# First-batch head pairs on the casting queue, and w_out with two rows to a partition

## The chip, the core and the metric

The kernel runs on one NeuronCore of a Trainium2 chip. Times are device microseconds (us) of that core. The kernel before was timed in 7 runs: median 297.09 us, lowest 295.44, highest 298.5. The profile shows one execution of its own, which took 297.81 us; its span, from the first to the last instruction that the profiler records, is 296.0 us.

## What is computed

Attention with 16 extra "beacon" keys that every query sees, then a feed-forward block with a product instead of a non-linearity, over 8 batches, 8 heads of width 64 and 576 positions:

```python
B, H, S, Nb, D = (8, 8, 576, 16, 64)
k_all = np.concatenate([beacon_k, k], axis=2)
v_all = np.concatenate([beacon_v, v], axis=2)
scores = scale * np.matmul(q, k_all.transpose(0, 1, 3, 2))
causal[:, Nb:] = np.triu(np.ones((S, S), dtype=bool), k=1)
a = np.exp(scores - scores.max(-1)) ; a /= a.sum(-1) + 1e-09
x = matmul(a, v_all).transpose(0, 2, 1, 3).reshape(B * S, H * D)     # 4608 x 512
out = ((x @ w1) * (x @ w2) @ w3) @ w_out                             # DF = 1024
```

Inputs and output are float32 in HBM; the kernel multiplies in float16. Since nothing stands between `w3` and `w_out`, the kernel forms their product once (`Wt`, 1024 x 512) and multiplies by that.

## The kernel before

**One list sets everything.** The string `ORDER` is a list of some 1,200 small operations. The last loop of the kernel goes through it and calls a function for each word, under a manual schedule: each engine executes its instructions exactly in the order in which the list gives them, and semaphores hold only what depends on other engines. So the list is also the order of the DMA queues. There is no planner at build time.

**The words.** `lq b c`, `lk b c`, `lkb b`, `lv b c`, `lvb b` load queries, keys, beacon keys, values, beacon values of batch b. `l1 c`, `l2 c`, `l3 r`, `lo a` load pieces of w1, w2, w3 and w_out; each piece is 512 KB of float32 in HBM and 256 KB as float16 on the chip. `t3 r` transposes a block of 128 rows of w3 on the PE, `e3` copies it out of PSUM, `f r a` multiplies it with piece a of w_out (two matmuls of 512 columns), and after `f r 0` to `f r 3` `ew r` writes block r of `Wt`. `tq`/`tk` are PE transposes of queries and keys, `eq`/`ek` their copies out, `tn`/`en` the same for the beacon keys of batch 0, `s b g` the scores of group g (13 to a batch), `exp` the exponential, `m` the causal mask, `v` the product with the values, `n` the division, `x`/`ex` a PE transpose of the attention output and its copy, `TX` the same by a transposing DMA. `Dq`/`Dk` are transposing DMAs of queries and keys, used from batch 2 or 3 on. `a`, `b` are x @ w1 and x @ w2, `ea` and `eb` their copies and product, `o` the product with `Wt`, `eo` its copy, `st` the store. `spin n` issues n matmuls on zeros, whose result is not used.

**Two queues of loads.** [...] Loads on the POOL queue write float16 from float32. At most eight POOL loads are under way: each waits for the landing of the one eight before it. The two queues share the 16 DMA engines.

**Batch 0 is loaded differently.** A head pair c (heads 2c and 2c+1) of q or k comes as one transfer of 96 partitions, each with six consecutive positions of both heads. In the kernel before all eight such transfers (`lq 0 c S`, `lk 0 c S`, 288 KB each) are float32 on SP, into the eight slots of `st8`, one slot each (`NOWN` = 8). `cast` on DVE (line 394) turns a slot into float16 with the heads side by side, `tq`/`tk` (line 406) then need six transposes to a pair. Slots 4 to 7 serve one more purpose: the first 128 columns of each hold the transposed block 2 of w3 (`HELD`, lines of `wT`), from `e3 2` until `f 2 0` to `f 2 3` have read slots 4, 5, 6, 7 in turn. So the last four pairs, `lk 0 2`, `lk 0 3`, `lq 0 2`, `lq 0 3`, stand in the list behind these, one by one.

**What is asked for at the start.** Before the first `f` the list issues on SP: `lq 0 0`, beacon keys, `lk 0 1`, `lk 0 0`, `lq 0 1`; and on POOL, behind the preparation of an identity and two masks: beacon values, `lo 0`, `lo 1`, `l3 0`, `l3 1`, `l3 2`, `l3 5`, `lo 2`, `lo 3`, `l3 3`.

Of the kernel before, what the change touches and what calls it, by code (L numbers as in the profile page):

```python
# [9 lines left out]
FP16 = mybir.dt.float16  # L10
AF = mybir.ActivationFunctionType
ALU = mybir.AluOpType
ds, ts = bass.ds, bass.ts
# [49 lines left out]
consts 0; consts 1; consts 2; spin 8 7; lq 0 0 S; lkb 0; lk 0 1 S; lk 0 0 S; lq 0 1 S; lvb 0; lo 0;  # L63
lo 1; cast 0 0 q; castb A; l3 0; tq 0 0 6; tn 0 7; cast 0 1 k; l3 1; eq 0 0 A 6; en 0 D 7; l3 2;
tk 0 1 5; cast 0 0 k; l3 5; ek 0 1 A 5; spin 1 7; tk 0 0 6; lo 2; ek 0 0 A 6; lo 3; spin 3 7;
s 0 0 0; s 0 1 2; s 0 2 4; exp 0 0 0; cast 0 1 q; spin 1 7; tq 0 1 6; exp 0 1 2; m 0 0 0; l3 3;
eq 0 1 D 6; exp 0 2 4; m 0 0 1; spin 3 7; s 0 3 0; s 0 4 2; lv 0 1; exp 0 3 0; spin 1 7; s 0 5 4;
spin 2 7; t3 0 6; l3 4; exp 0 5 4; m 0 1 0; e3 0 D 6; exp 0 4 2; spin 2 7; t3 1 7; lv 0 4; m 0 1 1;
f 0 0 6; e3 1 D 7; f 0 1 6; lv 0 0; t3 2 5; f 1 0 7; e3 2 A 5; f 1 1 7; lv 0 3; t3 5 4; f 2 0 5;
e3 5 A 4; f 2 1 5; lk 0 2 S; lv 0 2; f 2 2 5; lk 0 3 S; f 5 0 4; lq 0 2 S; f 1 2 7; f 2 3 5; l1 1;  # L70
f 0 2 6; ew 2 A 5; lq 0 3 S; f 0 3 6; f 5 1 4; ew 0 A 6; l3 6; t3 3 5; f 5 2 4; e3 3 A 5;
cast 0 2 k; f 5 3 4; f 1 3 7; lk 1 4 P; ew 5 D 4; tk 0 2 6; ew 1 A 7; f 3 0 5; ek 0 2 D 6; f 3 1 5;
f 3 2 5; cast 0 3 k; f 3 3 5; tk 0 3 6; l2 3; ew 3 A 5; cast 0 2 q; t3 4 7; ek 0 3 A 6; tq 0 2 4;
e3 4 D 7; lq 1 0 P; eq 0 2 A 4; spin 1 5; f 4 0 5; cast 0 3 q; s 0 6 0; s 0 7 2; l3 7; exp 0 6 0;
f 4 1 5; lq 1 1 P; tq 0 3 6; f 4 2 5; exp 0 7 2; eq 0 3 D 6; v 0 0 1 7; l2 1; m 0 2 0; v 0 0 0 6;
n 0 0 1 7; v 0 2 0 4; s 0 8 0; s 0 9 2; l1 0; n 0 2 0 4; exp 0 8 0; v 0 1 1 7; n 0 0 0 6; f 4 3 5;
lq 1 4 P; n 0 1 1 7; exp 0 9 2; t3 6 6; lk 1 1 P; tk 1 4 4; ew 4 D 5; s 0 10 0; e3 6 A 6;
v 0 1 0 7; ek 1 4 D 4; s 0 11 2; s 0 12 4; lkb 1; n 0 1 0 7; exp 0 10 0; f 6 0 6; m 0 2 1; l2 2;
tq 1 0 7; f 6 1 6; m 0 3 0; exp 0 11 2; eq 1 0 D 7; f 6 2 6; v 0 2 1 7; lv 1 3; exp 0 12 4;
m 0 3 1; t3 7 3; n 0 2 1 7; lq 1 2 P; v 0 3 0 2; e3 7 A 3; v 0 3 1 5; n 0 3 0 2; tq 1 1 7; f 6 3 6;  # L80
l1 2; n 0 3 1 5; eq 1 1 A 7; x 0 0 4; x 0 4 3; ew 6 A 6; f 7 0 2; ex 0 0 D 4; x 0 2 7; ex 0 4 D 3;
x 0 1 6; lq 1 3 P; ex 0 2 A 7; x 0 3 5; ex 0 1 D 6; tq 1 4 4; f 7 1 2; ex 0 3 A 5; eq 1 4 D 4;
lk 1 0 P; f 7 2 2; tk 1 1 6; a 0 1 7; l2 0; ek 1 1 A 6; l1 3; f 7 3 2; ea 0 1 A 7; b 0 4 6;
ew 7 D 2; lk 1 2 P; a 0 0 7; lk 1 3 P; tq 1 2 5; ea 0 0 A 7; b 0 2 4; lk 2 0 P; eq 1 2 D 5;
a 0 2 7; lv 1 2; a 0 4 5; lv 1 0; ea 0 2 A 7; eb 0 2 4; tq 1 3 7; lv 1 1; tk 1 0 3; eq 1 3 A 7;
a 0 5 2; ek 1 0 D 3; b 0 0 7; lk 2 2 P; b 0 1 4; eb 0 0 7; lvb 1; a 0 6 3; eb 0 1 4; lq 2 2 P;
tk 1 2 7; ea 0 4 A 5; ea 0 5 D 2; a 0 3 4; lkb 2; ek 1 2 A 7; ea 0 6 D 3; tk 1 3 5; lq 2 3 P;
b 0 5 7; eb 0 4 6; ek 1 3 A 5; ea 0 3 D 4; lk 2 1 P; s 1 0 0; s 1 1 2; s 1 2 4; eb 0 5 7;
exp 1 0 0; lv 1 4; b 0 6 6; lq 2 0 P; exp 1 1 2; m 1 0 0; a 0 7 7; eb 0 6 6; lk 2 3 P; exp 1 2 4;
tk 2 2 3; m 1 0 1; b 0 3 6; lq 2 4 P; ek 2 2 D 3; ea 0 7 A 7; lv 2 2; s 1 3 0; s 1 4 4; s 1 5 2;  # L90
eb 0 3 6; exp 1 3 0; lq 2 1 P; tk 2 0 7; tq 2 3 6; ek 2 0 D 7; exp 1 4 4; s 1 6 0; lk 2 4 P;
eq 2 3 D 6; v 1 0 0 7; m 1 1 0; lk 3 3 P; tk 2 1 6; n 1 0 0 7; exp 1 5 2; v 1 0 1 5; lv 2 1;
ek 2 1 D 6; v 1 1 0 4; tq 2 2 7; n 1 0 1 5; exp 1 6 0; Dk 2 3; tq 2 0 6; lv 2 3; tq 2 4 3; b 0 7 2;
n 1 1 0 4; eq 2 4 A 3; lk 3 0 P; eq 2 2 A 7; m 1 2 0; s 1 7 0; s 1 8 4; eq 2 0 D 6; exp 1 7 0;
lq 4 4 P; tq 2 1 3; m 1 1 1; v 1 2 0 7; lkb 3; eq 2 1 D 3; tk 2 4 6; exp 1 8 4; s 1 9 0; lq 3 2 P;
n 1 2 0 7; v 1 1 1 3; eb 0 7 2; o 0 3 7; lq 3 1 P; exp 1 9 0; n 1 1 1 3; lv 2 0; ek 2 4 A 6;
m 1 2 1; lvb 2; s 1 10 4; s 1 11 0; s 1 12 2; m 1 3 0; eo 0 3 A 7; lq 3 0 P; exp 1 10 4; v 1 3 0 6;
Dk 3 3; o 0 1 7; n 1 3 0 6; st 0 3 P; exp 1 12 2; lv 2 4; Dk 3 0; lq 3 3 P; exp 1 11 0; x 1 0 6;
eo 0 1 D 7; x 1 4 5; v 1 2 1 4; Dq 3 2; lk 3 4 P; ex 1 0 A 6; ex 1 4 D 5; o 0 2 3; n 1 2 1 4;
st 0 1 P; Dq 3 1; m 1 3 1; lk 3 2 P; v 1 3 1 7; eo 0 2 A 3; s 2 0 0; s 2 1 4; s 2 2 2; n 1 3 1 7;  # L100
lvb 3; exp 2 0 0; o 0 0 6; Dq 3 0; st 0 2 P; exp 2 1 4; m 2 0 0; lk 3 1 P; exp 2 2 2; x 1 3 7;
m 2 0 1; x 1 2 5; x 1 1 4; ex 1 3 D 7; s 2 3 0; s 2 4 2; lv 3 1; ex 1 2 D 5; ex 1 1 A 4; v 2 0 0 7;
eo 0 0 D 6; exp 2 4 2; a 1 3 5; n 2 0 0 7; exp 2 3 0; a 1 1 6; Dq 3 3; lq 3 4 P; ea 1 3 D 5;
s 2 5 2; s 2 6 4; s 2 7 0; ea 1 1 A 6; m 2 1 0; lv 3 4; Dk 3 4; exp 2 6 4; v 2 1 0 7; b 1 1 6;
lv 3 2; n 2 1 0 7; exp 2 5 2; m 2 2 0; v 2 0 1 5; eb 1 1 6; v 2 2 0 7; exp 2 7 0; a 1 4 4; Dk 3 2;
lv 3 3; n 2 0 1 5; b 1 3 6; n 2 2 0 7; lv 3 0; ea 1 4 A 4; m 2 1 1; s 2 8 2; s 2 9 0; s 2 10 4;
lq 4 0 P; eb 1 3 6; exp 2 8 2; v 2 1 1 7; b 1 0 6; exp 2 9 0; Dk 3 1; m 2 2 1; lk 4 1 P; n 2 1 1 7;
a 1 0 3; exp 2 10 4; m 2 3 0; a 1 6 7; lkb 5; ea 1 0 D 3; v 2 2 1 5; eb 1 0 6; Dq 3 4; lq 4 2 P;
ea 1 6 A 7; v 2 3 0 4; n 2 2 1 5; a 1 7 6; lq 4 3 P; n 2 3 0 4; b 1 4 7; x 2 0 5; lk 4 3 P;
eb 1 4 7; x 2 4 4; a 1 5 3; ex 2 0 A 5; ex 2 4 D 4; ea 1 7 A 6; b 1 5 7; ea 1 5 D 3; lk 4 0 P;  # L110
s 2 11 0; s 2 12 4; s 3 0 2; eb 1 5 7; st 0 0 P; exp 2 11 0; Dq 4 4; b 1 6 6; lq 4 1 P; exp 3 0 2;
m 2 3 1; b 1 7 7; lkb 4; Dk 4 1; eb 1 6 6; exp 2 12 4; a 1 2 3; m 3 0 0; eb 1 7 7; Dq 4 2;
v 3 0 0 6; ea 1 2 A 3; s 3 1 0; s 3 2 4; s 3 3 2; n 3 0 0 6; exp 3 1 0; Dq 4 3; v 2 3 1 7; b 1 2 6;
exp 3 3 2; m 3 0 1; lv 4 3; Dq 4 0; n 2 3 1 7; s 3 4 0; s 3 5 2; lk 4 2 P; exp 3 2 4; m 3 1 0;
x 2 3 7; eb 1 2 6; lv 4 0; Dk 4 3; exp 3 5 2; x 2 1 5; x 2 2 4; ex 2 3 D 7; o 1 3 6; lk 4 4 P;
ex 2 1 D 5; ex 2 2 A 4; m 3 1 1; lvb 4; exp 3 4 0; lv 4 4; a 2 2 7; eo 1 3 D 6; Dq 4 1; lk 5 0 P;
s 3 6 2; s 3 7 4; s 3 8 0; ea 2 2 A 7; st 1 3 P; Dk 4 0; exp 3 6 2; v 3 0 1 6; a 2 0 7; lv 4 2;
n 3 0 1 6; exp 3 8 0; o 1 1 3; m 3 2 0; ea 2 0 D 7; exp 3 7 4; lq 5 3 P; m 3 2 1; tk 4 2 6;
eo 1 1 A 3; v 3 2 0 7; ek 4 2 D 6; v 3 1 1 5; lk 5 1 P; n 3 2 0 7; a 2 1 6; n 3 1 1 5; Dk 4 4;
st 1 1 P; v 3 1 0 7; ea 2 1 A 6; lv 4 1; s 3 9 0; s 3 10 2; s 3 11 4; n 3 1 0 7; exp 3 9 0;  # L120
lq 5 0 P; b 2 0 6; exp 3 10 2; m 3 3 0; o 1 2 7; eb 2 0 6; exp 3 11 4; v 3 2 1 6; m 3 3 1;
eo 1 2 A 7; v 3 3 0 5; n 3 2 1 6; st 1 2 P; b 2 2 7; n 3 3 0 5; b 2 1 6; eb 2 2 7; TX 3 0;
s 3 12 0; s 4 0 2; s 4 1 4; eb 2 1 6; exp 3 12 0; Dq 5 3; a 2 5 7; exp 4 0 2; v 3 3 1 6;
ea 2 5 D 7; Dk 5 1; s 4 2 0; s 4 3 2; lv 5 0; exp 4 1 4; m 4 0 0; b 2 5 7; n 3 3 1 6; lk 6 3 P;
TX 3 4; exp 4 3 2; m 4 0 1; v 4 0 0 5; a 2 6 6; lk 5 4 P; eb 2 5 7; exp 4 2 0; TX 3 1; lv 5 1;
m 4 1 0; a 2 4 4; ea 2 6 D 6; lk 5 2 P; v 4 1 0 7; n 4 0 0 5; TX 3 3; ea 2 4 A 4; s 4 4 2; s 4 5 0;
s 4 6 4; lv 5 3; n 4 1 0 7; exp 4 4 2; a 2 7 6; Dq 5 0; lq 5 4 P; exp 4 6 4; lvb 5; v 4 0 1 7;
ea 2 7 D 6; lq 5 2 P; b 2 7 3; TX 3 2; exp 4 5 0; n 4 0 1 7; lq 5 1 P; b 2 6 6; m 4 2 0; Dk 5 0;
m 4 1 1; v 4 2 0 7; lk 5 3 P; eb 2 7 3; b 2 4 5; Dk 5 4; n 4 2 0 7; a 2 3 4; eb 2 4 5; lv 5 2;
o 1 0 7; eb 2 6 6; ea 2 3 A 4; Dk 5 2; lq 6 3 P; b 2 3 6; eo 1 0 A 7; s 4 7 0; s 4 8 2; s 4 9 4;  # L130
eb 2 3 6; lq 6 2 P; exp 4 7 0; o 2 2 7; Dq 5 4; st 1 0 P; exp 4 8 2; exp 4 9 4; v 4 1 1 6; m 4 2 1;
eo 2 2 D 7; s 4 10 0; s 4 11 2; s 4 12 4; Dq 5 2; exp 4 10 0; n 4 1 1 6; st 2 2 P; o 2 1 7;
m 4 3 0; Dk 6 3; exp 4 12 4; exp 4 11 2; a 3 2 6; Dq 5 1; eo 2 1 D 7; a 3 4 5; st 2 1 P; m 4 3 1;
ea 3 2 A 6; Dk 5 3; a 3 1 6; ea 3 4 A 5; a 3 0 7; ea 3 1 A 6; b 3 4 6; v 4 3 1 5; Dq 6 3; eb 3 4 6;
# [56 lines left out]
def kernel(  # L191
# [13 lines left out]
    nc = tc.nc  # L205
    B, H, S, D = q.shape
# [475 lines left out]
```

## Time and profile before

| | |
|---|---|
| timed, median of 7 (lowest to highest) | 297.09 us (295.44 to 298.5) |
| profiled execution: time / span | 297.81 us / 296.0 us |
| busy DVE, ACT, POOL | 53%, 55%, 45% of the span |
| scores start on PE | 9.72 us |
| first product with the values (L523) | 34.42 us |
| first w1/w2 product (L564) | 46.58 us on the chain |
| last matmul record / end of span | 292.96 us / 296.0 us |
| HBM read / written | 39.32 MB / 9.44 MB |

PE is TensorE, PEld its weight loads, DVE VectorE, ACT ScalarE, POOL GpSimd, SP the queue of SyncE. Under "timeline" the profile lists instructions with their start; under "chain" it follows back from the last instruction what released each step; under "windows" it sums the busy time of each engine in a stretch, beside the TensorE clock that was granted there (1.00 is full) and what the DMA engines moved. A PE that is marked busy isn't necessarily useful: the `spin` matmuls (line 605) count too, and matmuls at half clock count double.

### The profile page before, as it was taken

Reading aid. Unit: us, or ns where it says so; the run is one execution under the profiler, and the core shown is the slowest. Engines: PE = TensorE matmul, PEld = TensorE weight load, DVE = VectorE, ACT = ScalarE, POOL = GpSimd, SP = SyncE. Lnnn points to the kernel's source line nnn. Section 1 sums busy time; section 2 is a strip of 40 time slices with the busy share of each in tenths; the row PEclk is TensorE's granted clock in tenths of the full one; section 3 lists DMA queues with packets and bytes.
Section 4 is the critical chain, followed back from the end, with each engine's and each line's share of the span. In section 5 each row is a group of like instructions: output and inputs, shape, how many; then the busy total and the mean of one; then the engine's idle time right before and its main releaser. Section 6 shows DMA issues by size and latency. Waiting matters only on the chain.

```text
span 296.0 us, 7052 instructions
## 1 busy us (share of the span) xinstructions
PE 287.8 (97%) x2914; PEld 157.4 (53%) x2914; DVE 156.1 (53%) x350; ACT 162.8 (55%) x211; POOL 133.0 (45%) x185
## 2 busy tenths in 40 slices
PE   7997999999999999999999999999999999999995
PEld 2453675565655556555545554565456444544443
DVE  5323582776677665773526655556676262430430
ACT  3653594498785886657436651765187233443232
POOL 8464688959865385583087820572001000201000
PEclk9998999999999999999999999999999999999999
DMA  7999999999999999999999995699923110331004
GB/s 173 204 191 243 191 172 169 148 140 85 181 174 136 179 129 174 131 128 158 186 195 138 168 168 145 72 149 174 123 70 103 27 38 0 112 86 71 35 30 150
DMA packets 153616, 39.56 MB, mean 134 GB/s; under 512 B 143216, under 2 KB 150128, under 8 KB 153584
## 3 DMA queue, kind: packets, MB, share of 16 engines
q0 software_dynamic: 114320, 26.86, 101.6%
q1 hardware_dynamic: 39264, 12.25, 27.8%
q8 instruction: 23, 0.38, 0.6%
q14 instruction: 9, 0.07, 0.1%
HBM read 39.32 MB, written 9.44 MB: 165 GB/s over the span
## 4 chain that ended last, share of the span: by engine, by line
PE 92%; DMA 4%; ACT 2%; DVE 1%; SPq 0%; issue 0%; DVEq 0%
PE one L564 42%; PE one L585 21%; PE one L523 10%; PE pair L492 9%; DMA st<-in_k_dram 4%; PE one L477 4%; ACT ring L502 2%; PE one L605 1%; PE one L412 1%; PE one L549 1%; PE one L468 1%; PE one L406 1%; DVE o16k L394 0%; SPq L345 0%; DVE gT L296 0%
## 5 line engine op out<-in xcount | busy, mean ns | idle before, releaser
L564 PE MATMUL one<-xT,w 128*128 128x512 f16 x576 | 133.2, 379 | 0.0
L502 ACT ACTIVATE ring<-pair 128x1024 f16<-128x1024 f32 x104 | 99.0, 1027 | 15.3 <-PE pair L492 14.9
L564 PEld LDWEIGHTS <-w 128*128 128x128 f16 x576 | 53.4, 98 | 59.8 <-issue 1.7
L579 DVE TENSOR_TENSOR gT<-one,asb 128x512 f16<-128x512 f32 x72 | 49.1, 690 | 56.9 <-PE one L564 32.9
L585 PE MATMUL one<-Wt,gT 128*128 128x512 f16 (+1 forms) x296 | 66.8, 373 | 0.0
L300 ACT ACTIVATE asb<-one 128x512 f32<-128x512 f32 x52 | 31.0, 597 | 64.9 <-PE one L564 34.1
L599 POOL DMA_DIRECT2D out_dram<-st x32 | 18.0, 564 | 93.0 <-ACT st L300 59.9
L334 POOL DMA_DIRECT2D va<-in_v_dram x40 | 34.1, 857 | 34.5 <-PE one L523 29.5
L585 PEld LDWEIGHTS <-gT 128*128 128x128 f16 x296 | 27.7, 98 | 30.2 <-issue 0.8
L523 PEld LDWEIGHTS <-ring 128*128 128x128 f16 x960 | 34.7, 98 | 9.4 <-issue 1.2
L523 PE MATMUL one<-va,ring 128*128 128x65 f16 x960 | 37.6, 193 | 0.0
L326 POOL DMA_DIRECT2D q<-in_q_dram x35 | 29.9, 856 | 10.6 <-PE one L412 3.2
L535 DVE TENSOR_TENSOR x<-one,rd 128x256 f16<-128x256 f32 (+1 forms) x64 | 31.4, 491 | 2.2
L334 POOL DMA_DIRECT2D k<-in_k_dram x35 | 29.7, 852 | 4.2 <-DMA k<-in_k_dram 1.5
L492 PE MATMUL pair<-qT,kT 64*128 64x80 f16 (+4 forms) x736 | 30.9, 227 | 0.2
L300 ACT ACTIVATE st<-one 128x512 f32<-128x512 f32 (+1 forms) x24 | 13.9, 579 | 31.2 <-PE one L585 31.2
L492 PEld LDWEIGHTS <-kT 64*128 64x128 f16 x736 | 20.7, 96 | 13.4 <-issue 9.1
L512 DVE TENSOR_TENSOR ring<-ring,MD 128x768 f16<-128x768 f16 x32 | 17.7, 553 | 11.4 <-ACT ring L502 11.4
L302 DVE TENSOR_SCALAR asb<-one 128x512 f32<-128x512 f32 x20 | 13.6, 688 | 8.8 <-PE one L564 8.7
L534 DVE RECIPROCAL rd<-one 128x4 f32<-128x4 f32 (+1 forms) x64 | 11.8, 184 | 10.8 <-PE one L523 10.3
L477 PE MATMUL one<-wo,gT 128*128 128x512 f16 x56 | 16.2, 410 | 0.4 <-DVE gT L296 0.4
L512 DVE TENSOR_TENSOR ring<-ring,MX 128x384 f16<-128x384 f16 x32 | 11.3, 352 | 8.7 <-ACT ring L502 8.7
(56 smaller groups left out, 133.2 us busy)
## 6 DMA issues: line engine op xcount, KB each, us to landing
out_dram<-st POOLq DMA_DIRECT2D x32, 256.0 KB, 5.9
q<-in_q_dram POOLq DMA_DIRECT2D x28, 128.0 KB, 6.8
va<-in_v_dram POOLq DMA_DIRECT2D x24, 128.0 KB, 7.5
k<-in_k_dram POOLq DMA_DIRECT2D x21, 128.0 KB, 7.3
xT<-in_moe_w_dram POOLq DMA_DIRECT2D x8, 256.0 KB, 9.7
w<-in_moe_w_dram POOLq DMA_DIRECT2D x8, 256.0 KB, 7.6
st<-in_q_dram SPq DMA_DIRECT2D x4, 288.0 KB, 7.2
st<-in_k_dram SPq DMA_DIRECT2D x4, 288.0 KB, 5.7
```

The source lines that it names most:

```text
L300: nc.scalar.activation(dst, src, AF.Copy, scale=by)
L326: nc.gpsimd.dma_start(dst[:rows, c], src[b, :, ds(c * P, rows), :].rearrange("h s d -> s h d"))
L334: nc.gpsimd.dma_start(dst[ds(p0, rows), c], src[b, :, ds(s0, rows), :].rearrange("h s d -> s h d"))
L477: nc.tensor.matmul(bank(n), wT(r)[:, a, rt % 2, :], wo16[:, rt, :], start=(rt == 0), stop=(rt == NFT - 1),)
L492: nc.tensor.matmul(shape(n, "pair")[:, hh, ds(col, w)], kT[ds(hh * 64, 64), t, ts(jt, P)], qT[ds(hh * 64, 64), t, ds(q0, w)],)
L502: nc.scalar.activation(held(b, g)[:, :, 0:GW], shape(n, "pair"), AF.Exp, scale=scale)
L512: nc.vector.tensor_tensor(blk, blk, msk, ALU.mult)
L523: nc.tensor.matmul(pv[:, 2 * at + hh, 0 : D + 1], held(b, g)[:, hh, ds(col, P)], va[:, jt, 2 * t + hh, 0 : D + 1], start=(jt == 0), stop=( ...
L535: nc.vector.tensor_tensor(x16s[b % NB2][:, ds(2 * h, ni), ts(t, P)].rearrange("p i (h d) -> p i h d", h=2), pv[:, 0 : 2 * ni, 0:D].rearran ...
L564: nc.tensor.matmul(bank(n), w12[:, kt, ds(i * DF + kf * P, P)], xT[:, kt, ds(mc * 512, 512)], start=(kt == 0), stop=(kt == NKT - 1),)
L579: nc.vector.tensor_tensor(gTs[mc % 2][:, kf, :], bank(n), asb[slot["asb", (mc, kf)]], ALU.mult)
L585: nc.tensor.matmul(bank(n)[:, 0:w], gTs[mc % 2][:, kf, ts(mt, P)], Wt[:, kf, ds(c0, w)], start=(kf == 0), stop=(kf == NFT - 1),)
```

## The change

Four things are edited.

1. Only `lq 0 0` and `lk 0 0` stay on SP (`NOWN` = 2: slots 0 and 1). The other six pairs of batch 0 are issued on POOL, so that they arrive as float16. They land in the second halves of slots 7, 6, 5, 4, 2, 3 (`spare`), which the held block of w3 doesn't touch. `cast` stays, now from where the pair landed (`landed`), and can run on ACT or DVE; four of the eight are on ACT.
2. The beacon keys of batch 0 come as float16 on POOL directly into `b16`; the copy `castb` is gone.
3. A piece of w_out is read as two consecutive rows to a partition (4 KB in a run) instead of two rows 128 apart (2 KB runs). To match, `t3` takes every second column of w3.
4. The list is a new one: another order of loads, of work on every engine and of PSUM banks. It has 20 spins (22 before), 15 PE transposes of the attention output (16), 25 `TX` (24), 11 stores on SP (5).

```diff
-    NOWN = 8
+    NOWN = 2
...
-    wo_v = moe_w_out.rearrange("(a c p) n -> a p c n", p=P, c=2)
+    w3_v = w316.rearrange("p a c (r n e) -> p a c r e n", e=2, n=P)
+    wo_v = moe_w_out.rearrange("(a p c) n -> a p c n", p=P, c=2)
...
+    half = RUN * D
+    spare = [sts[i][:, half : 2 * half].bitcast(FP16) for i in (7, 6, 5, 4)]
+    spare += [sts[i][:, half : 2 * half].bitcast(FP16) for i in range(NOWN, 4)]
+    landed = {}
...
         if b == 0:
-            nc.sync.dma_start(
-                sts[take("own", (z, c), NOWN)][:NR].rearrange("p (h n) -> p h n", h=2),
-                src[b, ds(2 * c, 2)].rearrange("h (p j) d -> p h (j d)", j=RUN),
-            )
+            pair = src[b, ds(2 * c, 2)].rearrange("h (p j) d -> p h (j d)", j=RUN)
+            if e == "S":
+                land, queue = sts[take("own", (z, c), NOWN)], nc.sync
+            else:
+                land, queue = spare.pop(0), nc.gpsimd
+            queue.dma_start(land[:NR].rearrange("p (h n) -> p h n", h=2), pair)
+            landed[z, c] = land
...
-    def cast(b, t, z):
+    def cast(b, t, z, e="D"):
...
-            nc.tensor.transpose(pt[:, rt, :], w316[:, r // 2, r % 2, ts(rt, P)], ident)
+            nc.tensor.transpose(pt[:, rt, :], w3_v[:, r // 2, r % 2, rt // 2, rt % 2], ident)
```

The list up to the first product with the values, before (masks, copies and divisions partly left out here):

```
consts; spin 8; lq 0 0 S; lkb 0; lk 0 1 S; lk 0 0 S; lq 0 1 S; lvb 0; lo 0; lo 1; l3 0; tq 0 0; tn 0;
l3 1; l3 2; tk 0 1; l3 5; spin 1; tk 0 0; lo 2; lo 3; spin 3; s 0 0; s 0 1; s 0 2; spin 1; tq 0 1;
l3 3; spin 3; s 0 3; s 0 4; lv 0 1; spin 1; s 0 5; spin 2; t3 0; l3 4; spin 2; t3 1; lv 0 4; f 0 0;
f 0 1; lv 0 0; t3 2; f 1 0; f 1 1; lv 0 3; t3 5; f 2 0; f 2 1; lk 0 2 S; lv 0 2; f 2 2; lk 0 3 S;
f 5 0; lq 0 2 S; f 1 2; f 2 3; l1 1; f 0 2; lq 0 3 S; f 0 3; f 5 1; l3 6; t3 3; f 5 2; cast k2; f 5 3;
f 1 3; tk 0 2; f 3 0; f 3 1; f 3 2; cast k3; f 3 3; tk 0 3; cast q2; t3 4; tq 0 2; spin 1; f 4 0;
cast q3; s 0 6; s 0 7; f 4 1; tq 0 3; f 4 2; v 0 0 1
```

and after:

```
lq 0 0 S; lk 0 0 S; lo 0; spin 8; l3 3; lkb 0 P; l3 2; l3 0; cast q0 on ACT; l3 1; lo 2; spin 1;
tq 0 0; cast k0 on ACT; lo 1; spin 2; tk 0 0; lk 0 1 P; spin 7; t3 3; lo 3; tn 0; lq 0 2 P; s 0 0;
s 0 1; s 0 2; lq 0 3 P; f 3 0; t3 2; lq 0 1 P; t3 0; t3 1; lk 0 2 P; f 2 0; f 0 0; lv 0 4; f 1 0;
f 0 1; l3 6; f 0 2; cast k1 on ACT; l3 5; f 3 1; f 3 2; f 1 1; lvb 0; f 3 3; f 0 3; cast q2; l3 4;
tk 0 1; f 2 1; f 2 2; lv 0 3; cast q3; f 2 3; lk 0 3 P; tq 0 3; tq 0 2; f 1 2; lv 0 0; f 1 3; cast q1;
cast k2 on ACT; tq 0 1; lv 0 2; spin 1; tk 0 2; lv 0 1; spin 1; s 0 3; s 0 4; s 0 5; t3 5; t3 6;
s 0 6; f 5 0; t3 4; f 5 1; s 0 7; f 5 2; cast k3; f 4 0; tk 0 3; f 6 0; f 4 1; f 6 1; v 0 2 0
```

The rest of the list, for the other batches and the feed-forward block, has the same operations with the same tiles in another order.

## The prediction

> **What bounds the kernel now.** I read the page first: which engine is full, and where it isn't.
>
> ```profile
> PE 287.8 (97%) x2914; PEld 157.4 (53%) x2914; DVE 156.1 (53%) x350; ACT 162.8 (55%) x211; POOL 133.0 (45%) x185
> ...
> PEclk9998999999999999999999999999999999999999
> ```
>
> The PE is the only full engine, so time can come only from stretches where it waits, spins or runs at a reduced clock. The one dent in the clock is in the fourth slice. The stretches, by the windows (PE, PEld, DVE, ACT, POOL busy, then granted clock, DMA share, GB/s):
>
> ```profile
> 0.00:13.40 13.40, 11.09 (x71) 4.88 (x72) 6.34 (x21) 6.67 (x8) 8.87 (x20) 1.00 0.93 187
> 13.40:24.70 11.30, 11.30 (x99) 6.12 (x97) 2.18 (x5) 7.06 (x8) 7.39 (x10) 1.00 1.58 199
> 24.70:32.70 8.00, 5.51 (x38) 2.72 (x37) 4.18 (x7) 2.26 (x4) 2.82 (x5) 0.79 1.41 231
> 32.70:292.90 260.20, 259.91 (x2713) 143.66 (x2712) 143.35 (x319) 146.37 (x190) 113.97 (x152) 1.00 1.31 125
> ```
>
> From 32.7 us on only 0.29 us are idle: nothing is to be had there, only to be lost. What stands before is told by the chain of waits (start, length, step):
>
> ```profile
> 2.22 5.00 DMA st<-in_k_dram
> ...
> 19.66 6.47 DMA st<-in_k_dram
> ...
> 26.26 0.57 DVE o16k L394
> 26.87 0.66 PE one L406 x6
> 27.53 3.11 PE one L477 x8
> ...
> 34.59 1.37 PE one L523 x42
> ```
>
> Two waits for a key pair carry the opening. The second one, `lk 0 2`, is issued only at 19.66, behind `f 2 0`, lands at 26.14, and leaves the PE idle from 24.7 to 26.87; after that eight `f` matmuls take 3.11 us, where the chain has 0.86 for four at full clock, so 1.4 us more are lost.
>
> **The yardstick.** I compare the start of the first product with the values, 34.59 us. By the list, the PE work before it is:
>
> - before: 6 `t3`, 23 `f`, 8 `tq`/`tk`, `tn`, 8 `s`, 22 spins
> - after: 7 `t3`, 23 `f`, 8 `tq`/`tk`, `tn`, 8 `s`, 20 spins
>
> At full clock, by the chain's rows, a `t3` is 0.45 us, an `f` 0.43, six transposes 0.26, `s 0 0` to `s 0 2` 0.77, all eight `s` 2.1. That makes 2.7+9.9+2.1+0.1+2.1 = 16.9 us of work within 34.59; 17.7 us are waits, spins and half clock.
>
> **The loads, step by step.** I take each transfer's issue and landing from the trace.
>
> Pieces of weights on POOL land at 10.00, 11.28, 12.53, 13.79, 15.04, 16.29: 1.26 us each for 512 KB read and 256 KB written. Float32 pairs on SP land at 5.95, 7.21, 8.04 (1.26 and 0.83 for 288 KB), and in the second round, mixed with POOL's, at 26.14, 27.66, 29.52, 31.57: 1.5 to 2.0 each. In that round two value tiles on POOL take over 3 us each (23.63 to 27.02 to 30.08), where they otherwise take 0.86 to 0.88.
>
> [...] The rows show that the written bytes are what is paid for: about 200 KB a us in POOL's casts (256 KB in 1.26) and 230 to 250 in SP's uncast pairs, although POOL reads twice as many. So a pair as float16, 144 KB, is **estimated** at 0.72 us. [...] The larger part is order: nothing is held behind `f 2` any more.
>
> - `lq 0 0`: first as before, lands at 4.17.
> - `lk 0 0`: next on SP, without beacon keys and `lk 0 1` ahead of it: 4.17 + 1.2 = 5.4 (before 7.21).
> - POOL issues `lo 0` first, at about 0.8 instead of 3.06, ahead of identity and masks. Before, it landed 1.96 us behind the last SP pair (8.04 to 10.00); now 5.4 + 1.8 = 7.2. The identity moves behind one issue of 0.73 us, to about 2; it is needed at 5.0.
> - Then one queue: `l3 3` 8.45, beacon 8.6, `l3 2` 9.85, `l3 0` 11.1, `l3 1` 12.35, `lo 2` 13.6, `lo 1` 14.9, `lk 0 1` 15.6, `lo 3` 16.9, `lq 0 2` 17.6, `lq 0 3` 18.3, `lq 0 1` 19.05, `lk 0 2` 19.75, `lv 0 4` 20.1, `l3 6` 21.4, `l3 5` 22.6, `l3 4` 24.0, `lv 0 3` 24.9, `lk 0 3` 25.6, and the other three value tiles until 28.2.
>
> POOL's issues (0.55 to 0.88 us each, unchanged in kind) stay ahead: the ninth waits for `lo 0` at 7.2, with seven transfers still queued. Edit 3's longer runs: pieces of w_out land 1.28 apart, of w3, whose rows are 4 KB already, 1.25, so at most 4 x 0.03 us. Nothing taken.
>
> **The PE, step by step.**
>
> - `cast` of q0 on ACT: between the rows 128x576 (0.64) and 128x1024 (1.01), so 0.8; 5.0. `tq` at half clock 0.66, copy by DVE 0.76.
> - k0: cast until 6.2, spins until 6.5, `tk` 7.15, seven spins at 0.43 until 10.15, `t3 3` and `tn` until 11.3 at half clock or 10.7 at full, beacon copy, `s` from about 11.7. The copies are hidden by the seven spins.
> - `s` 0.77, `f 3 0`, three `t3` until 14.3. The weights for these lie there 1.5 us or more earlier.
> - Copies of `w3` blocks bind now: ACT has three exponentials (1.02 each) before `e3 1`, so `f 0 0` starts at about 15.65 and `f 1 0` at 16.3; 1.0 us lost.
> - Then 12 `f` and five transposes, each pair landed at least 1 us before its cast: until 22.9. ACT carries `eq`, the cast of k2 (0.8), `eq` in a row, so `s 0 3` waits until 23.9. DVE's three casts until there are hidden by `f`s.
> - Three `s`, two `t3`, `s 0 6`, `f 5 0`, `f 5 1`, `t3 4`, `s 0 7`, `f 5 2`, `f 4 0`, `tk 0 3`, three `f`: 23.9 to 30.2, with 0.5 us lost to copies. The values landed at 28.2, so the PE, not the queue, sets this.
>
> 34.59 - 30.2 = 4.4 us. One `t3` more is done by then (0.45), one PE transpose of x is gone (0.2): **5.0 us** if the clock is full from about 10. Two costs come off.
>
> *The clock.* In the trace it became full at 13.4 us, after a stretch that was spins, scores and six transposes. [...]
>
> *The later list.* It is new on all engines. Before, the idle waits of the PE after 32.7 sum to 0.29 us; there is no row for the new order. Bounds: 0.3 better, 3 worse (one more wait like that at 24.7, with its cold stretch, is 3.5). Its DMA lead is larger than before by some 2 us. I take 0.3.
>
> *Column steps of two in `t3`'s weights.* No row shows one. The load of 128 columns is hidden at 30 ns a piece under L523's short matmuls (0.91 us for 30); doubled it is 61 against 56 of a transpose: 64 x 5 ns = 0.3. The worst price is PEld's 98 ns unhidden, 64 x 42 = 2.7. I take 0, by the near row.
>
> Sum: 5.0 - 0.7 - 0.3 = 4.0. The profiled execution took 297.81, so it would take 293.8; the median of the seven is 0.7 lower: 297.1 - 4.0 = **293.1 us**. The tail (two half stores, 3.1 us from the last matmul) is the same.
>
> **Rivals.**
>
> [...]
> 2. *The wait only moves.* In the lists of landings and of PE work above, `lo 1`, `lo 3`, `lk 0 2`, `lk 0 3` land 1 to 3 us before their use; a queue slower by 10% to 25% eats the gain up: 295.6 to 298.6. Against: in the trace 1.25 to 1.28 us for five pieces in a row, without spread.
> 3. *Slower: one queue for everything.* Place: POOL's queue from `lo 0` (7.2) to the last value tile (28.2), 21 us. Price: the yardstick follows the last value tile. It passes 35.2 (34.59 and the 0.65 already done) if the queue takes 28 us, 1.33 times as much; from there the kernel is slower, at 1.5 times it ends near 301, with idle stretches that drop the clock again. For: value tiles at 3.2 us each in the mixed stretch; against: that stretch had SP's float32 pairs beside, which are gone.
>
> **How the numbers follow.** Forecast 0.68, 291.3 to 294.8; rival 1 0.13; rival 2 0.08; rival 3, with a bad later list, 0.11. The range for eight in ten is 291.0 to 295.8: it takes in the forecast and rival 1. What can be told from no change is about 0.5%, 295.6 to 298.6. Faster 0.81, same 0.08, slower 0.11.
>
> **What would show it.** Right: no DMA wait of more than 1 us on the chain after 6 us; no PE idle stretch over 1 us after 10; L523 first near 30; POOL's weight pieces still 1.26 apart; pairs on POOL about 0.7. Wrong: a second dent in the clock after 15 us; a first L523 later than 33; PE idle after that of over 1.5 us; `t3` (now on the line of the transposes of w3) over 0.6 us for eight.

## The result, and the profile after

| | before | changed |
|---|---|---|
| timed, median | 297.09 us | 292.78 us |
| lowest to highest (runs) | 294.3 to 300.9 (31) | 291.87 to 294.89 (12) |
| profiled execution: time / span | 297.81 / 296.0 us | 293.03 / 291.3 us |
| first product with the values | 34.42 us | 28.91 us |
| first w1/w2 product | 46.41 us | 41.60 us |
| from the first values product to the start of the last matmul | 258.22 us | 259.07 us |

The ratio is 0.9865, with an interval of 0.9839 to 0.9892: 1.35% faster. In a later set of runs the same kernel had 294.44 us against 296.29, a ratio of 0.9915 (0.9881 to 0.9949): the gain between the medians is 4.3 us in the first set and 1.85 us in the second. Ratios leave out single runs that lie over 1.5% above the fastest of their kernel, so a ratio can differ from the quotient of two medians.

The page of the changed kernel, busy time and granted clock:

```profile
PE 283.7 (97%) x2908; PEld 153.2 (53%) x2908; DVE 152.4 (52%) x342; ACT 165.7 (57%) x217; POOL 133.3 (46%) x186
...
PEclk9999999999999999999999999999999999999999
```

The PE is busy for 4.1 us less, and the dent in the fourth slice is gone. The same stretches as before, by the windows (PE, PEld, DVE, ACT, POOL busy, granted clock, DMA share, GB/s):

```profile
0.00:13.40 13.40, 11.11 (x94) 5.46 (x94) 5.16 (x19) 8.33 (x9) 9.41 (x23) 1.00 0.94 185
13.40:24.70 11.30, 10.32 (x109) 5.56 (x108) 4.90 (x9) 6.44 (x10) 8.76 (x13) 1.00 1.41 195
24.70:32.70 8.00, 7.98 (x117) 4.87 (x118) 6.30 (x16) 4.71 (x7) 6.85 (x9) 1.00 2.09 169
32.70:288.20 255.50, 254.26 (x2594) 137.31 (x2591) 136.04 (x300) 145.84 (x193) 108.27 (x143) 1.00 1.37 126
```

The third row holds most of the gain. Before, the PE was idle there for 2.49 of 8 us at a mean clock of 0.79; now it is idle for 0.02 us at full clock, and does 117 matmuls where it did 38. The first row gains too, at equal busy time: 94 matmuls instead of 71. The last row gives something back: 1.24 us idle, where it was 0.29.

How often a run has such a dent, in this place or another, can be read from the mean granted clock of the timed runs. 3.41 us at half clock, as in the profile of before, lower the mean by 0.006 (0.5 x 3.41 / 296). All twelve runs of the changed kernel have 0.999 or 1.0, and ten of the twelve in the later set 0.998 or more. Of 72 runs of the kernel before, timed beside the experiments, 59 have 0.994 or less. What a dent costs in a typical run these numbers don't show: within the kernel before, the runs without one aren't faster (medians of 296.6, 297.3 and 296.4 us in three sets, against 296.5, 297.1 and 296.2).

The instructions of the opening, by the timeline (start, length, engine and line, tiles, count; in brackets the idle time before and what ended it), and one later row:

```profile
1.26 3.89 PE L620 MATMUL one<-zeros 128*128 128x512 f16 x9 [1.26 <-DVE zeros L624]
...
4.11 0.83 ACT L296 CAST o16q<-st 96x768 f16<-96x768 f32 x1 [2.02 <-DMA st<-in_q_dram]
...
5.00 0.43 PE L421 MATMUL one<-ident,o16q 96*128 96x96 f16 x6
...
17.24 1.02 PE L492 MATMUL one<-wo,gT 128*128 128x512 f16 x4 [0.86 <-DMA wo<-in_moe_w_out_dram]
...
17.52 0.36 DVE L296 COPY o16q<-st 96x768 f16<-96x768 f16 x1 [4.70 <-DMA st<-in_q_dram]
...
28.91 0.53 PE L538 MATMUL one<-va,ring 128*128 128x65 f16 x12
...
96.05 0.54 PE L538 MATMUL one<-va,ring 128*128 128x65 f16 x12
```

The six transposes at 5.00 take 0.43 us, not the 0.66 that such a group took at half clock before (at 26.87): the clock is already full, by its record from 4.9 us on. A DVE cast's 4.70 us of idle time before 17.52 were spent waiting for a pair; the PE had other work. The one real stop of the PE after its start is at 17.24, for `lo 3`. The list of everything that the PE waited for (total, times, longest) says the same:

```profile
PE one L620 <- DVE zeros L624: 1.3, 1, 1.3
PE one L492 <- DMA wo<-in_moe_w_out_dram: 0.9, 1, 0.9
PE pair L507 <- DMA kT<-k: 0.8, 1, 0.8
PE pair L507 <- DVE kT L296: 0.4, 1, 0.4
PE one L427 <- DMA q<-in_q_dram: 0.3, 1, 0.3
```

Apart from the start, no wait reaches 1 us. The 0.8 us for `kT` lies at 114 us.

### The profile page after: what moved, and what is told of

Read it like the earlier page. It is cut to its first block, busy times and chain, and to the rows that moved or that the text cites. A ratio compares the mean times of both kernels' runs of the same rounds, so it can differ in the third digit from the quotient of the medians.

```text
span 291.3 us, 7022 instructions
## 1 busy us (share of the span) xinstructions
PE 283.7 (97%) x2908; PEld 153.2 (53%) x2908; DVE 152.4 (52%) x342; ACT 165.7 (57%) x217; POOL 133.3 (46%) x186
## 4 chain that ended last, share of the span: by engine, by line
PE 73%; DMA 15%; POOL 7%; issue 1%; SPq 1%; DVE 1%; ACT 0%; POOLq 0%; ACTq 0%
PE one L579 37%; PE one L600 20%; PE one L538 8%; PE pair L507 7%; DMA w<-in_moe_w_dram 5%; DMA wo<-in_moe_w_out_dram 3%; DMA kT<-k 3%; DMA xT<-in_moe_w_dram 2%; DMA q<-in_q_dram 2%; POOL q L332 2%; POOL k L340 2%; POOL va L340 1%; POOL w L389 1%; SPq L470 1%; PE one L564 1%
## 5 line engine op out<-in xcount | busy, mean ns | idle before, releaser
L300 ACT ACTIVATE asb<-one 128x512 f32<-128x512 f32 x53 | 31.7, 597 | 56.3 <-PE one L579 48.2
L614 POOL DMA_DIRECT2D out_dram<-st x26 | 14.9, 572 | 67.7 <-ACT st L300 35.1
L340 POOL DMA_DIRECT2D va<-in_v_dram x40 | 34.7, 874 | 22.1 <-PE one L538 14.3
L538 PEld LDWEIGHTS <-ring 128*128 128x128 f16 x960 | 35.3, 97 | 11.1 <-issue 2.6
L300 ACT ACTIVATE st<-one 128x512 f32<-128x512 f32 (+1 forms) x28 | 16.3, 582 | 36.8 <-PE one L600 36.8
L340 POOL DMA_DIRECT2D k<-in_k_dram x35 | 30.3, 872 | 7.0 <-DMA va<-in_v_dram 4.8
L332 POOL DMA_DIRECT2D q<-in_q_dram x35 | 30.5, 880 | 6.1 <-DMA k<-in_k_dram 3.1
L507 PEld LDWEIGHTS <-kT 64*128 64x128 f16 x736 | 19.0, 95 | 14.6 <-issue 10.4
L527 DVE TENSOR_TENSOR ring<-ring,MD 128x768 f16<-128x768 f16 x32 | 17.7, 553 | 13.2 <-ACT ring L517 13.1
L492 PE MATMUL one<-wo,gT 128*128 128x512 f16 x56 | 14.9, 380 | 1.2 <-DMA wo<-in_moe_w_out_dram 0.9
L302 DVE TENSOR_SCALAR asb<-one 128x512 f32<-128x512 f32 x19 | 13.0, 688 | 2.7 <-PE one L579 2.4
```

Of the source, the lines that this page charges most:

```text
L300: nc.scalar.activation(dst, src, AF.Copy, scale=by)
L332: nc.gpsimd.dma_start(dst[:rows, c], src[b, :, ds(c * P, rows), :].rearrange("h s d -> s h d"))
L340: nc.gpsimd.dma_start(dst[ds(p0, rows), c], src[b, :, ds(s0, rows), :].rearrange("h s d -> s h d"))
L492: nc.tensor.matmul(bank(n), wT(r)[:, a, rt % 2, :], wo16[:, rt, :], start=(rt == 0), stop=(rt == NFT - 1),)
L507: nc.tensor.matmul(shape(n, "pair")[:, hh, ds(col, w)], kT[ds(hh * 64, 64), t, ts(jt, P)], qT[ds(hh * 64, 64), t, ds(q0, w)],)
L527: nc.vector.tensor_tensor(blk, blk, msk, ALU.mult)
```

## The experiments

Each profile was read with the yardstick of the prediction, the start of the first product with the values, and with what follows it: the time from there to the start of the last matmul. Edit 2 (the beacon keys) and the casts on ACT were not tested by themselves.

### Edit 1 undone in the new list: six pairs back on SP

The changed list, letter by letter, but the six pairs come as float32 on SP, in four slots; a slot is used again after its cast.

```diff
-    NOWN = 2
+    NOWN = 4
-    lk 0 1 P ... lq 0 2 P ... lq 0 3 P ... lq 0 1 P ... lk 0 2 P ... lk 0 3 P
+    lk 0 1 S ... lq 0 2 S ... lq 0 3 S ... lq 0 1 S ... lk 0 2 S ... lk 0 3 S
```

> The changed kernel with the six pairs back on SP as float32 at their places in the new list, in four slots (a slot is reused after its cast). My theory: two of them are issued at about 2 us and two more at about 6, and push the weights back by 4 us or more: 295.5 to 297.5. Rival, that the new order alone makes the gain: 292.5 to 293.3.

Measured: 296.67 us, ratio 0.9988 (0.9958 to 1.0018). The gain is gone, as expected. The windows of this kernel:

```profile
0.00:13.40 13.40, 9.48 (x68) 4.35 (x69) 3.33 (x16) 5.92 (x7) 7.95 (x20) 0.90 0.93 215
13.40:24.70 11.30, 9.14 (x71) 4.93 (x69) 4.11 (x8) 5.24 (x8) 5.52 (x7) 0.96 1.24 226
24.70:32.70 8.00, 7.63 (x98) 4.48 (x97) 6.29 (x12) 6.64 (x8) 7.03 (x9) 1.00 2.09 169
...
33.30:291.30 258.00, 257.73 (x2675) 140.13 (x2673) 138.67 (x308) 147.56 (x195) 109.09 (x144) 1.00 1.34 125
```

In the first 24.7 us the DMA engines move more (215 and 226 GB/s against 185 and 195), and the PE does fewer matmuls, 139 against 203. SP issues two of the pairs at 1.75 and 2.24 us, and five of the six land ahead of `lo 3`, where in the changed kernel one does. They take the place of weights: `l3 2` lands at 11.74 instead of 8.99, `lo 3` at 21.28 instead of 17.19. The PE waits for these, by its list of waits (total, times, longest):

```profile
PE one L477 <- DMA xT<-in_moe_w_dram: 2.6, 2, 1.7
...
PE one L486 <- DMA wo<-in_moe_w_out_dram: 1.1, 2, 0.8
```

The clock is at half from 10.85 to 14.26 (0.90 and 0.96 in the first two rows). The first values product starts at 33.33, 4.4 us later than in the changed kernel. So in the new list the gain of the opening needs the six pairs in POOL's queue as float16; the new order alone has none of it.

Queue and type are changed together here, and the landings say which part is the larger one. The last value tile comes at 29.43 instead of 28.10, and the loads of batch 1 behind it are 1.2 to 1.5 us later: by the end of the opening no more delay than that is left of the 864 KB more (6 x 144). The other 3 us of the 4.4 come with what landed first, and with the half clock behind those waits.

The last row is one to remember. From the first values product on, this kernel has the same list as the changed one. Here the PE idles for 0.27 us in it, and the stretch takes 258.0 us; in the changed kernel it idles for 1.24 us, and the stretch takes 259.1. The later list in itself has hardly a cost. It has one for a PE that arrives there 4.4 us earlier, while its loads don't: the last value tile of batch 3, on which more is said below, lands at 95.28 here and at 95.91 in the changed kernel, though it was issued 3.4 us later here.

### Edit 1 alone, in the list of before

Three steps: the last four pairs as float16 on POOL at their old places; the same directly behind `lo 3`; and, for the place without queue and type, as float32 on SP at an early place (`NOWN` = 4).

```diff
-    f 2 1; lk 0 2 S; lv 0 2; f 2 2; lk 0 3 S; f 5 0; lq 0 2 S; ... lq 0 3 S
+    f 2 1; lk 0 2 P; lv 0 2; f 2 2; lk 0 3 P; f 5 0; lq 0 2 P; ... lq 0 3 P     (same places)
+    lo 3; lk 0 2 P; lk 0 3 P; lq 0 2 P; lq 0 3 P; spin 3                        (early on POOL)
+    eq 0 1; lk 0 2 S; lk 0 3 S; lq 0 2 S; lq 0 3 S; exp 0 2                     (early on SP)
```

> The kernel before with its own list; only lk 0 2, lk 0 3, lq 0 2, lq 0 3 are issued on POOL as float16, each at its old place in the list. My theory: they are no longer held by f 2, but queue behind the values; the value tiles lose the stretch of 3 us each, k2 lands about 25; the idle stretch at 24.7 shrinks by 1 us or so: 295.3 to 296.3. Rival, that the queue and type are worth nothing without the new list: 297.1.

> The same as the one above, with these four pairs issued directly behind lo 3 in POOL's order. My theory: they land by about 22, the idle stretch of 2.1 us at 24.7 and the 1.4 us at half clock behind it are gone, the other loads are 3 us later and have the room: 293.7 to 294.7. Rival, that only the new order of the PE's work makes the gain: 296.5 or more.

> The kernel before with four slots for the pairs instead of eight (the later four reuse the slots of the first four), so that lk 0 2, lk 0 3, lq 0 2, lq 0 3 are issued on SP as float32 as soon as the first four are cast, from 5 to 9 us, and not behind f 2. My theory: written bytes are paid for, so these four take 4 to 5 us of the DMA engines ahead of the weights; the first t3 and f wait instead, near 15 us: 295.8 to 297.5. Rival, that only the place behind f 2 was at fault and not the type and the queue: 293.7 to 294.7, as with the cast.

| | median us | ratio (interval) | first values product | from there to the start of the last matmul |
|---|---|---|---|---|
| before, profile | 296.54 | | 34.42 | 258.22 |
| same places, POOL | 295.80 | 0.9977 (0.9948 to 1.0007) | 32.07 | 258.22 |
| early, POOL | 294.77 | 0.9928 (0.9898 to 0.9957) | 31.49 | 258.22 |
| early, SP | 295.33 | 0.9969 (0.9938 to 1.0) | 31.46 | 258.22 |

At the old places the PE still stops for `lk 0 2`, but for 1.84 us and at a clock that stays full (1.0 over the profile). By the timelines of the kernel before and of this one:

```profile
26.87 0.66 PE L406 MATMUL one<-ident,o16k 96*128 96x96 f16 x6 [2.11 <-DVE o16k L394]
...
26.12 0.43 PE L404 MATMUL one<-ident,o16k 96*128 96x96 f16 x6 [1.84 <-DVE o16k L392]
```

Early on POOL the stop is gone; the four pairs land at 20.29, 21.08, 21.74 and 22.47, 0.7 to 0.8 apart. Early on SP the stop is gone too, while `lo 3` lands at 21.96 instead of 19.06 before, and the w3 pieces ahead of it come 1.8 to 1.9 us apart. So in the old list asking for the pairs early is enough to remove the second wait, whatever the queue; freeing them from `f 2` at their old places isn't. Of the three expectations the first came true; the second was missed by 0.07 us; the third was missed, as the `t3` and `f` waited for no weights longer than 0.3 us, and the median lies between the theory's range and the rival's. That float16 on POOL is better than float32 on SP for these four pairs is not shown: the intervals overlap, the two profiles have the same yardstick, and the last value tile lands earlier with the pairs on SP (28.35 against 28.82). The last column shows how good the yardstick is: with the old list behind it, it is the same to 0.01 us in four kernels. The medians gain less than the yardsticks (0.7 to 1.8 us against 2.4 to 3.0); the profiled execution of before, at 297.81, lay above its median.

### The opening and the rest, each without the other

The new list up to the first values product with the rest of the old one, and the reverse.

```diff
-    ...; f 4 1; f 6 1; v 0 2 0; <rest of the new list>
+    ...; f 4 1; f 6 1; v 0 2 0; <what is not yet done, in the order of the old list>
```

> The changed kernel with its new list up to the first product with the values (and the blocks of Wt begun there finished), then what is left of the old list in the old order. The profiles say that the opening gained 5.5 us and the span 4.7, so my theory is that the later list gives back about 1: 291.5 to 292.3. Rival, that the later list is neutral and the difference is scatter of the opening: 292.8.

> The counterpart: the kernel before with its own list up to the first product with the values, then what is left of the new list in the new order. My theory: no gain, 297.1 plus 0.5 to 1.3. Rival, that part of the gain lies in the later list: below 296.5.

Both are slower than both kernels: 299.39 us, ratio 1.0098 (1.0064 to 1.0132), and 299.37 us, 1.0124 (1.0069 to 1.0179). The first has a new stop at the seam, by its timeline:

```profile
36.97 0.32 PE L421 MATMUL one<-ident,k 80*128 80x80 f16 x4 [2.70 <-DMA k<-in_k_dram]
```

The keys of batch 1 are asked for too late for a PE that comes early, and the clock is at half from 37.3 to 44.1 us. The experiment misses its aim: it doesn't give the worth of the opening, but shows that an order of work and an order of loads hold only together. In the reverse kernel the first values product comes later than in either (36.39); by its list one `t3` and three `f` more stand ahead of it, 1.7 us at full clock.

### Without the late spins

The changed kernel with its first nine spins only; eleven are left out.

```diff
-    tk 0 0 7; ek 0 0 A 7; lk 0 1 P; spin 7 6; t3 3 6; lo 3; ...
+    tk 0 0 7; ek 0 0 A 7; lk 0 1 P; t3 3 6; lo 3; ...
```

> The changed kernel with the first nine spins alone; the other eleven (two, seven, one, one) are left out. Theory that the seven hold up the clock: in executions in which it did not rise early it comes later, so the median is 0.5 to 2 us higher (293.3 to 294.8), with a wider spread. Rival, that they only fill a wait for copies and loads: 292.3 to 293.0.

Measured: 293.8 us, ratio 0.9903 (0.9864 to 0.9941). The windows show what the seven spins hold up (the column before the last two is the clock):

```profile
5.10:8.40 3.30, 1.53 (x25) 1.13 (x24) 0.76 (x1) 1.51 (x3) 2.84 (x7) 1.00 1.12 181
8.40:11.90 3.50, 3.14 (x36) 2.02 (x34) 0.75 (x2) 2.92 (x4) 2.05 (x5) 0.51 1.12 209
11.90:20.00 8.10, 7.84 (x65) 4.33 (x63) 3.28 (x7) 4.58 (x7) 5.08 (x8) 1.00 1.29 201
```

Without them the PE is busy for 1.53 of the 3.30 us of one stretch, and in the next the clock is at 0.51. But the spins cost what they save: the first values product starts at 28.51 here and at 28.91 with them, and the time can't be told from that of the changed kernel. The spread is wider, as expected: 291.66 to 298.14 us, with three of eleven runs above 296. Why isn't known; this profile has a wait for a late load as well, of which the next two experiments tell.

### w_out's rows apart again

```diff
-    wo_v = moe_w_out.rearrange("(a p c) n -> a p c n", p=P, c=2)
+    wo_v = moe_w_out.rearrange("(a c p) n -> a p c n", p=P, c=2)
-    w3_v[:, r // 2, r % 2, rt // 2, rt % 2]
+    w316[:, r // 2, r % 2, ts(rt, P)]
```

> The changed kernel with its w_out pieces read again as two rows 128 apart (2 KB runs) and w3 transposed in adjacent columns. My theory: the four pieces cost 0.03 us more each and the weight loads of the transposes are hidden either way, so within 0.4 us of the changed kernel (292.8). Rival, that the longer runs carry part of the gain: 293.5 or more. Rival, that column steps of two cost weight-load time: 291.8 or less.

Measured: 295.23 us over six runs, ratio 0.9869 (0.9806 to 0.9932). The runs fall in two groups, three at 292.58 to 293.36 and three at 297.1 to 298.34, which says nothing of w_out. The upper three have a mean granted clock of 0.988 to 0.994, the lower three 1.0. The profiled one is of the upper group, and its list of waits begins with

```profile
PE one L538 <- DMA va<-in_v_dram: 3.6, 1, 3.6
```

a value tile of batch 3, used at 96 us, far from w_out. This asked for two more questions: is that wait the changed kernel's own, and is edit 3 worth anything once it is away?

### The changed kernel again, and its values first

The changed kernel itself, and three kernels beside it: the value tiles of batch 3 that follow `lv 3 2` placed directly behind it in POOL's queue; the same with w_out's rows apart; and the first with `lo 3` ahead of `lk 0 1` and two transposing DMAs exchanged as well.

```diff
-    lv 3 2; ...; lv 3 4; ...; lvb 3; ...; lv 3 0; ...; lv 3 1; ...; lv 3 3
+    lv 3 2; lv 3 4; lvb 3; lv 3 0; lv 3 1; lv 3 3; ...                  (values first)
-    tk 0 0; lk 0 1 P; spin 7; t3 3; lo 3    ...    Dq 4 2 ... Dk 4 4
+    tk 0 0; lo 3; lk 0 1 P; spin 7; t3 3    ...    Dk 4 4 ... Dq 4 2    (and more)
```

> The changed kernel itself once more, beside the others on one chip. Theory of the late value tile: most executions 292 to 293, some 296 to 298. Rival, that only the kernel with w_out's rows apart is caught by it: none over 295.

> The changed kernel; in POOL's order the value tiles of batch 3 (lv 3 4, lvb 3, lv 3 0, lv 3 1, lv 3 3) stand directly behind lv 3 2, ahead of loads of batch 4 and a store. In the profile of the changed kernel the last of them landed at 95.91 us and its first use was at 96.05; with w_out's rows apart it landed at 100.22 and the PE waited 3.6 us. Theory, that in some executions this wait takes back what the opening gained: no execution over 294.5, median 292.0 to 292.7. Rival, that the two groups of times come from elsewhere: still executions of 296 to 298, median as that of the changed kernel.

> The kernel with the value tiles of batch 3 first, and w_out's rows apart as before. Theory that the rows are worth nothing: within 0.5 us of the one with the value tiles first alone, and no executions over 294.5. Rival, that the longer runs do help: 0.7 us or more slower.

> The kernel with the value tiles of batch 3 first; besides, lo 3 stands ahead of lk 0 1 (the PE waited 1.0 us for lo 3 at 16 us), and Dk 4 4 changes places with Dq 4 2 (it waited 0.9 us for keys of batch 4 at 114 us). Theory, that both waits go: 0.8 to 1.8 us below the one with the value tiles first alone. Rival, that another load is late in their place: no difference.

| | median us (lowest to highest) | ratio (interval) | first values product | from there to the start of the last matmul |
|---|---|---|---|---|
| changed, again | 294.44 (291.73 to 296.4) | 0.9915 (0.9881 to 0.9949) | 29.02 | 260.30 |
| values first | 292.89 (291.83 to 295.41) | 0.9899 (0.9855 to 0.9942) | 28.67 | 258.76 |
| values first, rows apart | 293.12 (292.55 to 296.75) | 0.9899 (0.9867 to 0.9931) | 29.09 | 262.61 |
| values first, and more | 292.33 (292.09 to 297.14) | 0.9867 (0.9833 to 0.99) | 29.17 | 259.23 |

The twelve runs of the changed kernel don't fall into two groups as expected; they spread from 291.73 to 296.4 us, five of them above 295. In its second profile the wait is there, by the timeline:

```profile
96.25 0.32 PE L538 MATMUL one<-va,ring 128*128 128x65 f16 x5
98.51 0.37 PE L538 MATMUL one<-va,ring 128*128 128x65 f16 x7 [1.94 <-DMA va<-in_v_dram]
```

In the first profile the same tile landed at 95.91, and the twelve products began at 96.05, without a wait (the last row of the timeline shown there). Here it landed at 98.47, 13.44 us after its issue, and the twelve were split into five and seven. The sixth product, the first that had to wait, began at 96.21 in the first profile, so the kernel had 0.3 us of slack at this place. In two profiles of the changed kernel the wait is 0 and 1.9 us, with w_out's rows apart 3.6. With the values first the wait is gone. In the third kernel a wait turns up in its place, by that one's list of waits:

```profile
PE pair L501 <- DMA kT<-k: 2.1, 1, 2.1
```

for transposed keys, whose DMA was issued at 85.12 and landed at 95.54; the clock is at half after it, from 97.4 to 100.8. So the stretch from 80 to 100 us is short of loads, and reordering one kind of them can move the risk to another. None of the three is clearly faster than the changed kernel: all four intervals overlap. That no run would lie above 294.5 us with the values first didn't come true (295.41, and 296.75 with the rows apart). In the last kernel the two waits that it aims at are down to 0.5 us or less, but its median is 0.56 us lower, not 0.8 to 1.8, and the first values product isn't earlier. For edit 3 the pair with values first tells: 292.89 with the rows together, 293.12 apart, the same ratio. Nothing of it can be measured, with intervals of 0.3 to 0.4% on either side.

## Why the prediction was right

The forecast was 293.1 us in a range of 291.0 to 295.8; measured were 292.78, and 294.44 in the later set. For the profiled execution it was 293.8, and 293.03 came out. The mechanism was the one forecast: the second wait and the half clock behind it go, and the opening gets shorter. Two parts of the sum were off, in opposite directions. The opening gained 5.5 us (34.42 to 28.91) where 3.7 were forecast (34.59 to 30.9); the rest was to gain 0.35 (0.65 of work already done, less 0.3) and lost 0.85, or 2.1 in the second profile. That the total of the first set came so near to the forecast is partly luck: of the 4.0 us forecast, the later set has 1.85.

- **The second wait.** "Nothing is held behind `f 2` any more": right. Both the 2.49 us of idle time and the dent in the clock are gone. In the old list, removing this wait alone moved the first values product by 2.9 to 3.0 us of the 5.5. The kernel with six pairs back on SP loses the gain in another way, as no pair's slot waits for `f 2` there either.
- **The queue.** Right, within 0.9 us but for `lo 0`: `lk 0 0` landed at 5.16 (forecast 5.4), `lk 0 1` at 14.75 (15.6), `lo 3` at 17.19 (16.9), `lk 0 2` at 19.80 (19.75), the last value tile at 28.10 (28.2). `lo 0` came at 6.15 instead of 7.2. Two misses cancel here: the weights landed 0.8 to 1 us early, and from `lo 1` to `lk 0 2`, five pairs and `lo 3`, it took 5.79 us instead of 4.85.
- **The price of a pair.** Forecast 0.72 us; those that follow another pair landed 0.68, 0.76 and 0.85 us after it. The reading behind it was wrong: 288 KB in 1.26 and in 0.83 us are 229 and 347 KB a us, not 230 to 250. That written bytes are what is paid for isn't shown either. Six pairs uncast on SP made the last value tile 1.33 us later in the new list (six times 1.05 less 0.72, with 1.05 the mean of 1.26 and 0.83, would be an estimated 2), but four in the old list made it 0.47 us earlier. So the runs don't decide whether anything was to be had in DMA time. What the queue was worth lies mostly in the order of landing: with six pairs on SP the same list starts the first values product 4.4 us later, as SP's bytes landed ahead of POOL's weights. The prediction, too, had called order the larger part, but meant the hold behind `f 2`.
- **ACT's cast** 0.83 us (0.8). DVE's float16 copies of a pair, 0.35 to 0.74 us, had no figure in the sum, which took them as hidden by `f`; the PE didn't wait for one.
- **The PE to the first values product.** The scores started at 9.00 (forecast 11.7), `s 0 3` at 22.47 (23.9), the values at 28.91 (30.2 with a full clock from 10, 30.9 with the clock term). From `s 0 3` on it took 6.44 us, forecast 6.3.
- **The clock term, 0.7 us, was too large.** No run shows the 0.7: in the changed kernel's profile full clock was granted from 4.9 us on, ahead of the seven spins, and it never dropped: 0 lost. The scores started 2.7 us earlier than forecast; half of that was lost again until `s 0 3`; the longest wait on the way is the 0.86 us for `lo 3`. Rival 1 (half clock through the opening) did not happen in any of the seven profiles with this opening; without the late spins (8.4 to 11.9 us) or with six pairs on SP (10.85 to 14.26) some 3.4 us were at half.
- **The later list, 0.3 us, was too small.** 258.22 less the 0.65 of work already done makes 257.57; it took 259.07, so 1.5 us, and 2.7 in the profile of the later set. The bound of 3 held in these two; the profile with w_out's rows apart has 262.97, which is 5.4 us. The working had taken the earlier landings as a lead for what follows. But all pairs and values of batch 0 had landed 3.5 us earlier than before (28.10 against 31.57), while the PE was 5.5 us earlier, and it met the batch 3 loads at 80 to 100 us. Rival 2 (the wait only moves) is to that extent true: in the opening, where it was looked for, only as the 0.86 us for `lo 3`; 70 us later more, and only in some executions.
- **Edit 3** and the column step at nothing: not contradicted, by the pair of kernels above. Eight `t3` transposes have 0.61 us in the timeline with either, and also before the change; the 0.6 named as a sign against was set too close.
- **Rival 3** (one queue for everything): the queue took 22 us from `lo 0` (6.15) to the last value tile (28.10), where 28 were needed. It did not happen.
- **The signs.** A first values product near 30, pieces of weights about 1.26 us apart (1.22 to 1.38 between `l3 3` and `lo 1`) and no stop over 1 us after 10: as named in the first profile; the second has the 1.94 us at 98.5. "PE idle after that of over 1.5 us" as a sign against: 1.24 in the first profile, over 2.2 in the second, so this sign did appear there. One sign was badly put: no DMA of over 1 us on the chain after 6 us. The chain shows such steps, of the changed kernel (start, length, step):

```profile
2.34 5.27 DMA xT<-in_moe_w_dram
...
7.89 9.30 DMA wo<-in_moe_w_out_dram
...
20.11 2.60 POOL va L340 x3
...
24.58 7.03 DMA w<-in_moe_w_dram
```

The chain comes to these steps from a wait of the PE of 0.3 us, for queries at 60.97. From there it runs back along POOL's issues, several of which waited for an earlier landing (`lo 3` landed at 17.19, and POOL's next issue is at 17.48), and it gives each transfer's whole length, most of which other work covers. Length on the chain isn't time to be won; the list of the PE's waits says how much is.

## What to carry to other kernels

Look for loads that are late because of the buffer they land in: a transfer held behind the readers of a slot can cost its wait and half clock after it (here 2.11 us, and 3.41 us at half clock), and a smaller form of the data may fit where nothing holds it. When a transfer moves to another queue, ask first what it will land ahead of: here that was worth more than its bytes (some 3 us of the 4.4). And when an opening gets shorter, check every load further on by its slack (landing against use) in several executions: what was comfortable for a PE 5 us later may have 0.3 us left, and one profile won't show it.

## What the runs showed of the hardware that was not expected

- **The lengths of stretches at one clock were multiples of 3.41 us.** Between the first and the last change of the clock, the kernel before has 13.65 us at full (13.13 to 26.78), 3.41 at half (to 30.20) and 266.24 at full; the spliced one has 6.83 at half (37.28 to 44.11), the changed one 286.72 at full. The first record of full clock begins at 13.1 us in the kernel before and at 4.9 in the changed one. In the seven profiles that have the changed opening with its spins, no half clock followed in the opening, over transposes, spins and scores: four of them have a mean clock of 1.0, and the half clock of the other three lies at 37 us or later. The page prints 1.00 also where there is no record yet, so the duration of known matmuls has to be read beside it: 3.89 us for nine spins from 1.26 us on, 1.68 us for seven at 6.33.
- **Half clock followed some stops and not others.** It followed waits of 1.7, 2.1, 2.7 and 3.6 us (six pairs on SP, values first with rows apart, the spliced list, w_out's rows apart) and the 2.11 us of the kernel before, but not waits of 1.94 us (the second profile of the changed kernel, mean clock 1.0) and 2.6 us (a value tile at 96 us in the kernel without the late spins, mean clock 0.993, where a second stretch of 3.41 us at half beside that from 8.4 to 11.9 would give 0.988). So the length of a wait alone didn't tell. In the 3.41 us ahead of its half clock, the kernel before has 1.39 us of PE work (23.37 to 26.78); the kernel without the late spins has 1.53 in the 3.30 us ahead. In the changed kernel, counted in steps of 3.41 us from the first record of full clock to 288.2 us, the least is 2.56 us of work (15.12 to 18.54), and the clock stayed full. No run was made to test what decides.
- **The same transfer took up to twice as long.** Value tiles of 128 KB, with a median of 6.6 us from issue to landing, took 11.0 to 13.4 us between 78 and 96 us in the changed kernel, beside transposing DMAs of 7.5 to 10.2 us. With six pairs on SP, in the same later list, the last of them took 9.3 us. Why is open.
